# PReLU from PSUM, a one-column product as a tensor-scalar operation, and a new planned order of the first phase, in a pooled attention with feed-forward kernel

## The chip, the cores and the metric

The kernel runs on one core of a Trainium2 chip. The metric is the device time of one execution in microseconds (us). The engines are TensorE (PE; PEld is its weight load), VectorE (DVE), ScalarE (ACT), GpSimd (POOL) and SyncE (SP), which issues every DMA of this kernel. SBUF is the on-chip memory that all engines read; PSUM is the memory into which PE writes its products, in banks of 512 float32 columns.

## The reference

An attention whose keys and values are means of 8 neighbouring positions is followed by a feed-forward layer with PReLU (a slope `alpha` for each hidden feature).

```python
# q, k, v: (8, 8, 576, 64) float32
k_p = k.reshape(B, H, Sp, pool, D).mean(axis=3)      # pool = 8, Sp = 72
v_p = v.reshape(B, H, Sp, pool, D).mean(axis=3)
scores = scale * np.matmul(q, k_p.transpose(0, 1, 3, 2))
scores = scores - np.max(scores, axis=-1, keepdims=True)
attn = np.exp(scores)
attn = attn / (np.sum(attn, axis=-1, keepdims=True) + 1e-09)
x = np.matmul(attn, v_p)                             # then (4608, 512)

h = x @ w_in                                         # (512, 2048)
g = np.maximum(h, 0.0) + alpha * np.minimum(h, 0.0)
return (g @ w_out).astype(np.float32)                # (2048, 512)
```

## The kernel before

**Tiling.** The 4608 tokens are cut into nine chunks of 512 tokens. Every product is made of float16 halves: an operand is scaled by a power of two and split into a high part (ACT writes it) and a low part (what is left, written by DVE or POOL), and three matmuls of 512 columns give high x low, low x high and high x high. A chunk takes 192 matmuls `h` for the first layer (16 tiles `f` of 12), and 192 matmuls `o` for the second (4 token tiles `i`, each 16 steps of 3).

**The attention of a chunk** (`attention`): keys and values are pooled, scaled and split (`ks`, `kbd`, `vs`, `v`), queries are split (`q`), then come scores, row maxima, exponentials `e`, their normalisation (L532), the split into `apad` (L537 on ACT, L540 and L543 on POOL), a DMA transpose to `aT` for each of four token tiles, and the mix `x` (L605), which ACT and DVE split into the chunk's activation (L562, L566).

**The first layer of a tile** `f`: the matmuls fill one of two PSUM banks `h` (L769 to L771); ACT copies it, scaled by `rp`, to an SBUF tile `t` (L775), of which there are four, shared with `ks`, `vs` and the outputs; DVE makes the PReLU in place, the larger of `alpha` times `t` and `t` (L779); ACT writes its high part `g` (L786), POOL its low part (L789).

**The weights** arrive as 64-bit words, two words of 32 bits for each value, 8 tiles of 1 MB for each layer, into buffers `big`, of which there are twelve for all loads. `convert` turns a tile into float16 parts: ACT shifts the lower words (L641) and scales the upper ones into `v` (L651, L655; for three tiles of w1 POOL does it, L645), DVE joins three low bits (L665) and the sign (L669), each over 128 x 1024, ACT takes the high part (L688, L693), and POOL or DVE the low part (L707 on POOL for w1; L696 on DVE for 13 halves of w2, L702 on POOL for 3). The sign operation of every second tile frees a `big` buffer. No w2 low part can begin before the scale `s2` (L752), which needs the column maxima of all w2 tiles (L238), and so the last w2 load.

**What sets the order.** The first phase (`start`: chunk 0 as a whole, all weights, and the attention of chunk 1) is recorded in a `_Plan`: every operation has an engine, an assumed duration, what it comes after, buffers to take and give, and a rank from the table `RK`. The plan picks, engine by engine, what can start next and has the lowest rank, and issues the instructions in that order; PE gets idle matmuls where the plan sees a gap of more than 3.27 us. On the chip each engine runs its instructions in the issued order and waits for semaphores alone, not for planned times. For chunks 1 to 8 a loop issues the first layer with the next chunk's attention in between and then the second layer; there the compiler's scheduler sets the order, with second-layer products between first-layer tiles.

**What the change touches:** `RK`, `_Plan.add`, `start` and `emit`, `descale` (L581, the product of two scales and 2^-32 for each token, one column), `convert`, `scale_w1` (L718, L728), `ffn1_scaled`, `ffn1_prelu`, and the recording of the PReLU in `start`.

Of the kernel before, what the change touches and what calls it, by code (L numbers as in the profile page):

```python
# [72 lines left out]
class _Plan:  # L73
# [15 lines left out]
    def add(self, engine, us, emit, *after, rank=0.0, take=None, give=None):
        op = dict(engine=engine, us=us, emit=emit, after=after, rank=rank, n=len(self.ops),  # L90
                  take=take, give=(give,) if isinstance(give, str) else give or (), end=None)
        self.ops.append(op)
        return op

    def start(self, op, free):
        if any(d["end"] is None for d in op["after"]) or (op["take"] and not self.room[op["take"]]):
# [4 lines left out]
        return max(t)

    def emit(self):
        free, left = {}, list(self.ops)
        while left:
# [25 lines left out]
def pooled_attention_prelu_ffn(ctx: ExitStack, tc: tile.TileContext, qT, kT, vT, kN, vN, w1, w2, alpha, out):  # L131
# [441 lines left out]
    def descale(c, i):  # L573
# [4 lines left out]
        if key not in dss:  # L578
            ds = sml.tile([P, 1], F32, tag="ds", name="ds", bufs=4)
            for a, z, b in pr:  # L580
                nc.vector.scalar_tensor_tensor(out=ds[a:z], in0=eq[c, i // 2][a:z], scalar=2.0 ** -32,  # L581
                                               in1=ek[b][a:z], op0=ALU.mult, op1=ALU.mult)
# [50 lines left out]
    def convert(add, l, i, begin, sc, rank):  # L633
# [10 lines left out]
        if l == 1 and picked(i, RK["v_pool"], NF // 2):
            x = add("Pool", 2.4, lambda: nc.gpsimd.tensor_tensor(  # L645
                out=v(), in0=word(l, i, 1), in1=y1[:, 2 * i:2 * i + 2].broadcast_to([P, 2, 512]), op=ALU.mult),
                begin, rank=rank, take="v")
        elif l == 1:
            x = begin
            for j in range(2):  # L650
                x = add("ACT", 0.61, lambda j=j: nc.scalar.activation(  # L651
                    v()[:, j], word(l, i, 1)[:, j], AF.Copy, scale=y1[:, 2 * i + j:2 * i + j + 1]),
                    begin, x, rank=rank, take=None if j else "v")
        else:
            x = add("ACT", 1.15, lambda: nc.scalar.activation(  # L655
                v(), word(l, i, 1), AF.Copy, scale=2.0 ** -112 if wide else 1.0), begin, rank=rank, take="v")
        vi = lambda: v().bitcast(I32)
        if by_pool:
            x = add("Pool", 2.4, lambda: nc.gpsimd.tensor_tensor(
                out=vi(), in0=vi(), in1=eight.broadcast_to([P, 2, 512]), op=ALU.mult), x, rank=rank)  # L660
            x = add("DVE", 1.35, lambda: nc.vector.scalar_tensor_tensor(
                out=vi(), in0=word(l, i, 0).bitcast(I32), scalar=29, in1=vi(),
                op0=ALU.logical_shift_right, op1=ALU.bitwise_or), x, rank=rank)
        elif wide:
            x = add("DVE", 1.35, lambda: nc.vector.scalar_tensor_tensor(  # L665
                out=vi(), in0=vi(), scalar=3, in1=word(l, i, 0).bitcast(I32),
                op0=ALU.logical_shift_left, op1=ALU.bitwise_or), x, low, rank=rank)
        if wide:
            x = add("DVE", 1.5, lambda: nc.vector.scalar_tensor_tensor(  # L669
                out=vi(), in0=word(l, i, 1).bitcast(I32), scalar=-2 ** 31, in1=vi(),  # L670
                op0=ALU.bitwise_and, op1=ALU.bitwise_or), x, rank=rank, give="big" if i % 2 else None)
# [292 lines left out]
```

## Time and profile before

| what | us |
|---|---|
| median of three runs | 891.62 |
| lowest and highest of them | 888.89 and 892.07 |
| the profiled execution | 890.46 |
| its span, first to last instruction | 888.8 |
| PE, DVE, ACT, POOL busy in the span | 847.1, 452.9, 428.2, 400.5 |

The span has two parts that are read apart: the planned first phase, up to the mix of chunk 1, and the chunks after it. A mean over the whole span says little about either. A row of a group gives line, engine, operation, output and inputs with their shapes and the count, then busy us, mean ns of one, and the idle time ahead of it with what ended it. A row of the order in time gives start and duration in us; "x2" is two instructions merged into one row.

### The profile page before, as it was taken

Reading aid. Unit: us, or ns where it says so; the run is one execution under the profiler, and the core shown is the slowest. Engines: PE = TensorE matmul, PEld = TensorE weight load, DVE = VectorE, ACT = ScalarE, POOL = GpSimd, SP = SyncE. Lnnn points to the kernel's source line nnn. Section 1 sums busy time; section 2 is a strip of 40 time slices with the busy share of each in tenths; the row PEclk is TensorE's granted clock in tenths of the full one; section 3 lists DMA queues with packets and bytes.
Section 4 is the critical chain, followed back from the end, with each engine's and each line's share of the span. In section 5 each row is a group of like instructions: output and inputs, shape, how many; then the busy total and the mean of one; then the engine's idle time right before and its main releaser. Section 6 shows DMA issues by size and latency. Waiting matters only on the chain.

```text
span 888.8 us, 11503 instructions
## 1 busy us (share of the span) xinstructions
PE 847.1 (95%) x4447; PEld 411.1 (46%) x4447; DVE 452.9 (51%) x655; ACT 428.2 (48%) x724; POOL 400.5 (45%) x377
## 2 busy tenths in 40 slices
PE   6769997898999999999999999999999999999998
PEld 5444453344444544454445444544454444444443
DVE  4999999758415841583158315831583146112210
ACT  5967785555433643364336433643463346213330
POOL 1387948457714461456144614561456027202320
PEclk9879999999999999999999999999999999999999
DMA  9576312360621171117111611171115003100000
GB/s 339 198 158 268 124 51 51 75 202 9 157 96 40 25 182 56 39 28 192 43 39 28 178 57 38 29 198 37 39 28 119 36 13 70 26 36 12 1 25 24
DMA packets 93639, 74.75 MB, mean 84 GB/s; under 512 B 77040, under 2 KB 77616, under 8 KB 93584
## 3 DMA queue, kind: packets, MB, share of 16 engines
q1 hardware_dynamic: 93584, 74.01, 29.4%
q8 instruction: 35, 0.57, 0.3%
q14 instruction: 20, 0.16, 0.1%
HBM read 45.10 MB, written 9.44 MB: 61 GB/s over the span
## 4 chain that ended last, share of the span: by engine, by line
PE 81%; DVE 11%; POOL 3%; ACT 2%; DMA 2%; issue 2%; SPq 0%; POOLq 0%; ACTq 0%; DVEq 0%
PE o L815 13%; PE o L816 13%; PE o L817 13%; PE h L769 12%; PE h L770 12%; PE h L771 12%; PE x L605 2%; DVE v L665 2%; DVE t L779 2%; DVE m L238 1%; DMA vraw<-vT_dram 1%; PE s L595 1%; PE s L594 1%; PE s L596 1%; PE pl L283 1%
## 5 line engine op out<-in xcount | busy, mean ns | idle before, releaser
L789 POOL TENSOR_TENSOR g<-t,g 128x512 f16<-128x512 f32 x144 | 179.6, 1250 | 337.0 <-ACT g L786 337.0
L779 DVE SCALAR_TENSOR_TENSOR t<-t,al 128x512 f32<-128x512 f32 x144 | 140.5, 980 | 272.9 <-ACT t L775 266.1
L770 PE MATMUL h<-x,w 128*128 128x512 f16 x576 | 219.2, 381 | 2.4 <-DVE x L566 2.4
L769 PE MATMUL h<-x,w 128*128 128x512 f16 x576 | 219.1, 380 | 1.4 <-ACT o L805 1.4
L771 PE MATMUL h<-x,w 128*128 128x512 f16 x576 | 218.8, 380 | 0.0
L816 PE MATMUL o<-w,g 128*128 128x512 f16 x544 | 207.1, 381 | 4.4 <-POOL w L702 2.8
L815 PE MATMUL o<-w,g 128*128 128x512 f16 x544 | 206.7, 381 | 3.3 <-POOL g L789 2.8
L817 PE MATMUL o<-w,g 128*128 128x512 f16 x544 | 204.2, 381 | 0.0
L786 ACT CAST g<-t 128x512 f16<-128x512 f32 x144 | 88.4, 615 | 100.9 <-DVE t L779 100.5
L775 ACT ACTIVATE t<-h,rp 128x512 f32<-128x512 f32 x144 | 97.9, 681 | 67.1 <-PE h L771 63.7
L805 ACT ACTIVATE o<-o,os 128x512 f32<-128x512 f32 x34 | 23.2, 687 | 174.1 <-PE o L817 174.1
L815 PEld LDWEIGHTS <-g 128*128 128x128 f16 x576 | 56.5, 98 | 75.4 <-issue 6.0
L817 PEld LDWEIGHTS <-g 128*128 128x128 f16 x576 | 56.6, 98 | 73.8 <-issue 6.9
L771 PEld LDWEIGHTS <-w 128*128 128x128 f16 x576 | 56.5, 98 | 70.3 <-issue 3.5
L769 PEld LDWEIGHTS <-w 128*128 128x128 f16 x576 | 56.5, 98 | 68.1 <-issue 3.7
L816 PEld LDWEIGHTS <-g 128*128 128x128 f16 x576 | 56.5, 98 | 67.4 <-issue 2.1
L770 PEld LDWEIGHTS <-w 128*128 128x128 f16 x576 | 56.5, 98 | 65.4 <-issue 2.5
L463 POOL TENSOR_TENSOR vraw<-vraw 72x512 f32<-72x512 f32 (+1 forms) x56 | 58.9, 1069 | 56.7 <-DMA vraw<-vT_dram 45.8
L566 DVE SCALAR_TENSOR_TENSOR x<-x,xsc,x 128x512 f16<-128x512 f32 x36 | 25.8, 747 | 69.7 <-ACT x L562 69.7
L532 POOL TENSOR_TENSOR e<-e,sm 128x576 f32<-128x576 f32 x35 | 46.9, 1341 | 25.5 <-DVE sm L530 17.2
L537 ACT CAST apad<-e 128x576 f16<-128x576 f32 x72 | 44.8, 669 | 25.8 <-POOL e L532 18.0
L540 POOL TENSOR_TENSOR apad<-e,apad 128x448 f16<-128x448 f32 x36 | 41.7, 1158 | 3.3 <-ACT apad L537 3.1
(135 smaller groups left out, 886.0 us busy)
## 6 DMA issues: line engine op xcount, KB each, us to landing
w<-w_dram SPq DMA_DIRECT2D x16, 1024.0 KB
out_dram<-o SPq DMA_DIRECT2D x36, 256.0 KB
qraw<-qT_dram SPq DMA_DIRECT2D x17, 512.0 KB
vraw<-vT_dram SPq DMA_DIRECT2D x28, 288.0 KB
kraw<-kT_dram SPq DMA_DIRECT2D x12, 576.0 KB
kq<-kT_dram SPq DMA_DIRECT2D x2, 576.0 KB
nat<-kN_dram SPq DMA_DIRECT2D x2, 512.0 KB
nat<-vN_dram SPq DMA_DIRECT2D x2, 512.0 KB
```

The costliest lines, as they stand in the source:

```text
L463: nc.gpsimd.tensor_tensor(out=o, in0=y, in1=z, op=ALU.add)
L532: x = add("DVE" if i in on_dve else "Pool", us, lambda ex=ex, sm=sm, eng=eng: eng.tensor_tensor(out=ex(), in0=ex(), in1=sm().broadcast_to( ...
L769: nc.tensor.matmul(ps, w[:, 1, ks_], x[:, 0], start=(n == 0), stop=False)
L770: nc.tensor.matmul(ps, w[:, 0, ks_], x[:, 1], start=False, stop=False)
L771: nc.tensor.matmul(ps, w[:, 0, ks_], x[:, 0], start=False, stop=(n == NK - 1))
L775: nc.scalar.activation(t, hps.pop((c, f)), AF.Copy, scale=rp[:, f:f + 1])
L779: nc.vector.scalar_tensor_tensor(out=t, in0=t, scalar=al[:, f:f + 1], in1=t, op0=ALU.mult, op1=ALU.max)
L786: nc.scalar.copy(out=g[:, 0], in_=t)
L789: nc.gpsimd.tensor_tensor(out=g[:, 1], in0=t, in1=g[:, 0], op=ALU.subtract)
L815: nc.tensor.matmul(ps, g[:, 1, ts_], w[:, 0], start=(f == 0), stop=False)
L816: nc.tensor.matmul(ps, g[:, 0, ts_], w[:, 1], start=False, stop=False)
L817: nc.tensor.matmul(ps, g[:, 0, ts_], w[:, 0], start=False, stop=(f == NF - 1))
```

## The change

1. **PReLU.** ACT still copies `h`, scaled by `rp`, to `t`. DVE now takes its product from the PSUM bank itself, times a new column `ra` = `rp` x `alpha`, and the larger of that and `t` goes to `t`. The bank is so free only after the PReLU, where ACT's copy freed it. `ra` lies in the buffer of `m1`, and a POOL product for each of four groups of columns makes it.
2. **Scale product.** In `descale` the one-column product is a tensor-scalar operation, its second factor a scalar read from a column, where it was a scalar-tensor-tensor operation.
3. **Planner.** Every POOL operation and the DVE operations marked `two` (two tensors in SBUF, or a tensor-scalar form) share one `port`: in the plan one of them starts only when the last has ended. Many assumed durations are smaller.
4. **Table.** `RK` has new numbers. No scaling of w1 runs on POOL any more (`v_pool` was 3), four of eight w1 low parts run on DVE (`lo_dve` 0 to 4), all 16 w2 low halves run on DVE (`w2_dve` 13 to 16), and both halves of the early key pooling run on DVE (`k_pool` 1 to 0). A variant of `convert` that works in PSUM is added and is chosen for no tile (`ps1` and `ps2` are 0).

```diff
-RK = dict(k_pool=1, sh1_pool=0, sh2_pool=0, v_pool=3, s_pool=0, w2_dve=13, lo_dve=0, l1=392.23, step=2.57,
+RK = dict(k_pool=0, ps1=0, ps2=0, s_pool=0, w2_dve=16, lo_dve=4, l1=296.52, step=20.04, l2=536.5, mx1=19.17,
...
-    def add(self, engine, us, emit, *after, rank=0.0, take=None, give=None):
+    def add(self, engine, us, emit, *after, rank=0.0, take=None, give=None, two=False):
...
+                  two=two or engine == "Pool")
...
+        if op["two"]:
+            t.append(self.port)
         return max(t)
...
+            if op["two"]:
+                self.port = t + op["us"]
...
-                nc.vector.scalar_tensor_tensor(out=ds[a:z], in0=eq[c, i // 2][a:z], scalar=2.0 ** -32,
-                                               in1=ek[b][a:z], op0=ALU.mult, op1=ALU.mult)
+                nc.vector.tensor_scalar(out=ds[a:z], in0=eq[c, i // 2][a:z], scalar1=2.0 ** -32,
+                                        scalar2=ek[b][a:z], op0=ALU.mult, op1=ALU.mult)
...
-        if l == 1 and picked(i, RK["v_pool"], NF // 2):
-            x = add("Pool", 2.4, lambda: nc.gpsimd.tensor_tensor(
-                out=v(), in0=word(l, i, 1), in1=y1[:, 2 * i:2 * i + 2].broadcast_to([P, 2, 512]), op=ALU.mult),
-                begin, rank=rank, take="v")
...
-        x = add("DVE" if dve else "Pool", 1.5 if dve else 2.4, lambda: (nc.vector if dve else nc.gpsimd).tensor_tensor(
-            out=part(1), in0=v(), in1=part(0), op=ALU.subtract), x, rank=rank + RK[f"lo{l}"], give="v")
+        x = add("DVE" if dve else "Pool", 1.25 if dve else 2.3, lambda: (nc.vector if dve else nc.gpsimd).tensor_tensor(
+            out=part(1), in0=v(), in1=part(0), op=ALU.subtract), x, rank=rank + RK[f"lo{l}"], give="v", two=dve)
...
+        x = add("Pool", 0.2, lambda: nc.gpsimd.tensor_tensor(
+            out=rp[:, fs], in0=rp[:, fs], in1=sg[:, fs], op=ALU.mult), x, scaled["al"], rank=rank + 4)
         return y_, add("Pool", 0.2, lambda: nc.gpsimd.tensor_tensor(
-            out=rp[:, fs], in0=rp[:, fs], in1=sg[:, fs], op=ALU.mult), x, scaled["al"], rank=rank + 4)
+            out=ra[:, fs], in0=rp[:, fs], in1=al[:, fs], op=ALU.mult), x, rank=rank + 4)
...
-        nc.scalar.activation(t, hps.pop((c, f)), AF.Copy, scale=rp[:, f:f + 1])
+        nc.scalar.activation(t, hps[c, f], AF.Copy, scale=rp[:, f:f + 1])
...
-        nc.vector.scalar_tensor_tensor(out=t, in0=t, scalar=al[:, f:f + 1], in1=t, op0=ALU.mult, op1=ALU.max)
+        nc.vector.scalar_tensor_tensor(out=t, in0=hps.pop((c, f)), scalar=ra[:, f:f + 1], in1=t,
+                                       op0=ALU.mult, op1=ALU.max)
...
-            x = add("ACT", 0.69, lambda f=f: ffn1_scaled(0, f), x, rs[f], rank=rank + RK["sc"], take="f", give="h")
+            x = add("ACT", 0.69, lambda f=f: ffn1_scaled(0, f), x, rs[f], rank=rank + RK["sc"], take="f")
+            x = add("DVE", 0.76, lambda f=f: ffn1_prelu(0, f), x, rank=rank + RK["pre"], give="h")
             rd.append(x)
-            x = add("DVE", 1.25, lambda f=f: ffn1_prelu(0, f), x, rank=rank + RK["pre"])
```

The order moves at three places that matter below. Lines of the changed file differ: there L659 and L662 are the join and the sign operation, L775 is the PReLU, L701 the low part of w1, L712 the scale steps of w1, and `m_122` is the buffer of `m1` and `ra`.

First, POOL in the first phase, from its first product of the w1 scales on; `apad` is the split of a token tile of chunk 0. Before:

```order
L728 TENSOR_TENSOR rp<-rp,sg 128x2
L645 TENSOR_TENSOR v<-w_199,y_127 128x1024
L532 TENSOR_TENSOR e<-e,sm 128x576
L540 TENSOR_TENSOR apad_96<-e,apad_96 128x8x56
L543 TENSOR_TENSOR apad_96<-e,apad_96 128x8x16
L540 TENSOR_TENSOR apad_97<-e,apad_97 128x8x56
L543 TENSOR_TENSOR apad_97<-e,apad_97 128x8x16
L471 MEMSET vm 128x1
L728 TENSOR_TENSOR rp<-rp,sg 128x4
L707 TENSOR_TENSOR w_136<-v,w_136 128x2x512
L532 TENSOR_TENSOR e<-e,sm 128x576
L707 TENSOR_TENSOR w_136<-v,w_136 128x2x512
```

And in the changed kernel:

```order
L722 TENSOR_TENSOR rp<-rp,sg 128x2
L724 TENSOR_TENSOR m_122<-rp,al 128x2
L722 TENSOR_TENSOR rp<-rp,sg 128x4
L724 TENSOR_TENSOR m_122<-rp,al 128x4
L543 TENSOR_TENSOR apad_96<-e,apad_96 128x8x56
L546 TENSOR_TENSOR apad_96<-e,apad_96 128x8x16
L535 TENSOR_TENSOR e<-e,sm 128x576
L543 TENSOR_TENSOR apad_97<-e,apad_97 128x8x56
L546 TENSOR_TENSOR apad_97<-e,apad_97 128x8x16
L535 TENSOR_TENSOR e<-e,sm 128x576
L474 MEMSET vm 128x1
L701 TENSOR_TENSOR w_134<-v,w_134 128x2x512
```

The w1 scaling (L645) and one of the two w1 low parts (L707) ahead of the last tiles' splits are gone from POOL.

Second, DVE from the last split of chunk 0's activation on (`m_125`, and `m_123` after, are the maxima of w2 tiles, `w_272`, `w_282` tiles of w1). Before:

```order
L566 SCALAR_TENSOR_TENSOR x_688<-x,xsc,x_688 128x512
L238 TENSOR_REDUCE m_125<-w_664 128x2
L669 SCALAR_TENSOR_TENSOR v<-w_272,v 128x1024
L779 SCALAR_TENSOR_TENSOR t<-t,al 128x512
L238 TENSOR_REDUCE m_125<-w_686 128x2
L238 TENSOR_REDUCE m_125<-w_707 128x2
L779 SCALAR_TENSOR_TENSOR t<-t,al 128x512 x2
L238 TENSOR_REDUCE m_125<-w_732 128x2
L665 SCALAR_TENSOR_TENSOR v<-v,w_282 128x1024
```

And in the changed kernel, with `w_217` and `w_241` the fourth and fifth tile of w1 and `w_671` the first of w2:

```order
L569 SCALAR_TENSOR_TENSOR x_699<-x,xsc,x_699 128x512
L662 SCALAR_TENSOR_TENSOR v<-w_217,v 128x1024
L659 SCALAR_TENSOR_TENSOR v<-v,w_241 128x1024
L775 SCALAR_TENSOR_TENSOR t<-h,m_122,t 128x512
L662 SCALAR_TENSOR_TENSOR v<-w_241,v 128x1024
L712 TENSOR_SCALAR rp<-e_121 128x6
L241 TENSOR_REDUCE m_123<-w_671 128x2
L775 SCALAR_TENSOR_TENSOR t<-h,m_122,t 128x512
L241 TENSOR_REDUCE m_123<-w_697 128x2
L775 SCALAR_TENSOR_TENSOR t<-h,m_122,t 128x512
L241 TENSOR_REDUCE m_123<-w_717 128x2
L712 TENSOR_SCALAR y_125<-rp 128x6
```

At the split DVE now stands four joins and signs and three scale steps further back in the conversion of w1, and does them behind it.

Third, DVE in chunk 2, from the reduction of the next chunk's key maxima to the split of its queries. Before:

```order
L208 TENSOR_REDUCE pt<-pm 128x3
L213 TENSOR_SCALAR pr<-pt 128x3
L229 TENSOR_SCALAR e<-pr 128x3
L234 TENSOR_SCALAR s<-e 128x3
L581 SCALAR_TENSOR_TENSOR ds<-e 128x1
L581 SCALAR_TENSOR_TENSOR ds<-e 64x1 x2
L581 SCALAR_TENSOR_TENSOR ds<-e 128x1
L779 SCALAR_TENSOR_TENSOR t<-t,al 128x512
L425 SCALAR_TENSOR_TENSOR kbd_95<-ks,s,kbd_95 64x4x72 x2
L442 SCALAR_TENSOR_TENSOR q_2473<-qraw,s,q_2473 128x1024
L442 SCALAR_TENSOR_TENSOR q_2475<-qraw,s,q_2475 128x1024
```

And in the changed kernel:

```order
L216 TENSOR_SCALAR pr<-pt 128x3
L775 SCALAR_TENSOR_TENSOR t<-h,m_122,t 128x512
L232 TENSOR_SCALAR e<-pr 128x3
L237 TENSOR_SCALAR s<-e 128x3
L584 TENSOR_SCALAR ds<-e 128x1
L584 TENSOR_SCALAR ds<-e 64x1 x2
L584 TENSOR_SCALAR ds<-e 128x1
L428 SCALAR_TENSOR_TENSOR kbd_95<-ks,s,kbd_95 64x4x72 x2
L445 SCALAR_TENSOR_TENSOR q_2538<-qraw,s,q_2538 128x1024
L445 SCALAR_TENSOR_TENSOR q_2540<-qraw,s,q_2540 128x1024
L775 SCALAR_TENSOR_TENSOR t<-h,m_122,t 128x512
```

The PReLU that stood between the scale products and the key split has moved ahead of e, and the whole preparation of keys and queries now stands between two PReLUs.

Ahead of the mix of chunk 1, PE now has all 192 second-layer products of chunk 0; before, the last 12 of them stood behind it.

More of the change, by code (lines that the diff above doesn't have):

```diff
@@ L86, in __init__ @@
         self.fill = fill
-        self.ops, self.room = [], {k: n * [0.0] for k, n in room.items()}
-    def add(self, engine, us, emit, *after, rank=0.0, take=None, give=None):
+        self.ops, self.room, self.port = [], {k: n * [0.0] for k, n in room.items()}, 0.0
+    def add(self, engine, us, emit, *after, rank=0.0, take=None, give=None, two=False):
         op = dict(engine=engine, us=us, emit=emit, after=after, rank=rank, n=len(self.ops),
-                  take=take, give=(give,) if isinstance(give, str) else give or (), end=None)
+                  take=take, give=(give,) if isinstance(give, str) else give or (), end=None,
+                  two=two or engine == "Pool")
         self.ops.append(op)
@@ L428, in attention @@
                 h = add("ACT", 0.53, hi, scs[0], rank=rank)
-                kd.append(add("DVE", 0.6, lo, h, *kd[2 * i:], rank=rank, give="f" if j else None))
+                kd.append(add("DVE", 0.6, lo, h, *kd[2 * i:], rank=rank, give="f" if j else None, two=True))
         qd = {}
@@ L444, in attention @@
                     op0=ALU.mult, op1=ALU.subtract),
-                    h, *([qd[1]] if end else []), rank=rk,
+                    h, *([qd[1]] if end else []), rank=rk, two=True,
                         give="big" if end else "aT" if early and a + w == HC else None)
@@ L532, in attention @@
             x = add("DVE" if i in on_dve else "Pool", us, lambda ex=ex, sm=sm, eng=eng: eng.tensor_tensor(
-                out=ex(), in0=ex(), in1=sm().broadcast_to([P, 2, 4, SP]), op=ALU.mult), x, rank=rk)
+                out=ex(), in0=ex(), in1=sm().broadcast_to([P, 2, 4, SP]), op=ALU.mult), x, rank=rk, two=True)
             ev_ = lambda ex=ex: ex().rearrange("p b h s -> p (b h) s")
@@ L638, in convert @@
         v = once(lambda: wp.tile([P, 2, 512], F32, tag="v", name="v", bufs=ROOM["v"]))
-        by_pool = wide and picked(i, RK[f"sh{l}_pool"], NF // 2)
-        if wide and not by_pool:
-            low = add("ACT", 1.2, lambda: nc.scalar.activation(
+        ps = once(lambda: ps_s.tile([P, 2, CH], F32, tag="s", name="vw"))
+        by_ps = wide and picked(i, RK[f"ps{l}"], NF // 2)
+        u, kind = (ps, "S") if by_ps else (v, "v")
+        if wide:
+            low = add("ACT", 1.15, lambda: nc.scalar.activation(
@@ L650, in convert @@
             for j in range(2):
-                x = add("ACT", 0.61, lambda j=j: nc.scalar.activation(
-                    v()[:, j], word(l, i, 1)[:, j], AF.Copy, scale=y1[:, 2 * i + j:2 * i + j + 1]),
-                    begin, x, rank=rank, take=None if j else "v")
+                x = add("ACT", 0.66, lambda j=j: nc.scalar.activation(
+                    u()[:, j], word(l, i, 1)[:, j], AF.Copy, scale=y1[:, 2 * i + j:2 * i + j + 1]),
+                    begin, x, rank=rank, take=None if j else kind)
@@ L654, in convert @@
         else:
             x = add("ACT", 1.15, lambda: nc.scalar.activation(
[L656 to L667, printed above, removed]
@@ L668, in convert @@
-        if wide:
-            x = add("DVE", 1.5, lambda: nc.vector.scalar_tensor_tensor(
-                out=vi(), in0=word(l, i, 1).bitcast(I32), scalar=-2 ** 31, in1=vi(),
-                op0=ALU.bitwise_and, op1=ALU.bitwise_or), x, rank=rank, give="big" if i % 2 else None)
+                u(), word(l, i, 1), AF.Copy, scale=2.0 ** -112 if wide else 1.0), begin, rank=rank, take=kind)
+        if wide:
+            x = add("DVE", 1.22, lambda: nc.vector.scalar_tensor_tensor(
+                out=u().bitcast(I32), in0=u().bitcast(I32), scalar=3, in1=word(l, i, 0).bitcast(I32),
+                op0=ALU.logical_shift_left, op1=ALU.bitwise_or), x, low, rank=rank, two=not by_ps)
+            x = add("DVE", 1.22, lambda: nc.vector.scalar_tensor_tensor(
+                out=v().bitcast(I32), in0=word(l, i, 1).bitcast(I32), scalar=-2 ** 31, in1=u().bitcast(I32),
+                op0=ALU.bitwise_and, op1=ALU.bitwise_or), x, rank=rank, two=not by_ps,
+                take="v" if by_ps else None, give=(*(["big"] if i % 2 else []), *(["S"] if by_ps else [])))
@@ L718, in small @@
             return add("DVE", 0.2, lambda: nc.vector.tensor_scalar(
-                out=out, in0=in0, scalar1=s1, scalar2=s2_, op0=op0, op1=op1), x, rank=rank)
+                out=out, in0=in0, scalar1=s1, scalar2=s2_, op0=op0, op1=op1), x, rank=rank, two=True)
         x = add("DVE", 0.2, lambda: floor2(r[0], e1[:, fs], wide), x, rank=rank)
```

23 lines of the change are left out of this document (10 added, 13 removed).

## The prediction

> **What bounds the kernel now.** I read PE's busy slices first, then busy time by stage, then the chain of work that ended last, and then the groups of the first stage and its order in time.
>
> ```profile
> PE   6769997898999999999999999999999999999998
> 0.00:67.00 67.00, 44.68 (x251) 30.49 (x252) 52.67 (x99) 48.08 (x102) 32.29 (x35) 0.87 0.74 233
> 67.00:119.00 52.00, 47.85 (x234) 23.09 (x234) 49.90 (x52) 39.91 (x57) 42.88 (x25) 0.97 0.43 167
> 119.00:159.00 40.00, 33.26 (x190) 16.32 (x189) 39.63 (x50) 28.68 (x66) 27.56 (x27) 0.92 0.20 54
> 270.00:360.00 90.00, 90.00 (x487) 43.26 (x486) 43.47 (x63) 40.69 (x66) 39.31 (x41) 1.00 0.28 74
> ```
>
> A window row gives its bounds and length, then busy time of PE, PE's weight loads, DVE, ACT and POOL, and the granted clock. There are two regimes. From about 210 us on PE has no gap (90.00 of 90.00), so nothing that only shortens DVE, ACT or POOL work there can move the end. In the first phase DVE has no gap (49.90 of 52, 39.63 of 40), and PE waits for it. A gain must come from the first phase, up to the second mix:
>
> ```profile
> 63.23 1.93 PE L605 MATMUL x<-aT,v 88*64 88x512 f16 x16 [1.37 <-DVE v L665]
> 67.06 2.71 DVE L566 SCALAR_TENSOR_TENSOR x<-x,xsc,x 128x512 f16<-128x512 f32 x4
> 171.31 1.03 PE x L605 x12
> ```
>
> The first mix runs at 63.2, DVE splits its result at 67.1, and the mix of chunk 1 starts at 171.3. Behind that PE is full, and whatever 171.3 moves, the end moves.
>
> **Why DVE is full.** Much of its time is blocked time:
>
> ```profile
> L665 DVE SCALAR_TENSOR_TENSOR v<-v,w 128x1024 int32<-128x1024 int32 x16 | 25.4, 1589 | 0.0
> L669 DVE SCALAR_TENSOR_TENSOR v<-w,v 128x1024 int32<-128x1024 int32 x16 | 21.8, 1364 | 0.0
> L779 DVE SCALAR_TENSOR_TENSOR t<-t,al 128x512 f32<-128x512 f32 x16 | 17.7, 1129 | 0.4 <-ACT t L775 0.4
> L696 DVE SCALAR_TENSOR_TENSOR w<-v,s,w 128x512 f16<-128x512 f32 x13 | 15.1, 1174 | 0.9 <-ACT w L693 0.8
> 122.61 1.21 DVE L669 SCALAR_TENSOR_TENSOR v<-w,v 128x1024 int32<-128x1024 int32 x1
> 123.74 0.74 DVE L696 SCALAR_TENSOR_TENSOR w<-v,s,w 128x512 f16<-128x512 f32 x1
> 109.86 3.84 POOL L789 TENSOR_TENSOR g<-t,g 128x512 f16<-128x512 f32 x3
> 112.71 2.07 DVE L665 SCALAR_TENSOR_TENSOR v<-v,w 128x1024 int32<-128x1024 int32 x1
> ```
>
> The first four rows are means of the first 172 us. At 122.6, with POOL idle, the 1024 form takes 1.13 us from start to start and the 512 form 0.74. At 112.7 the same 1024 form stands at 2.07, since POOL's third g ends at 113.70; 1.08 us later it is done. So a DVE operation with both tensors in SBUF waits for POOL's running one. The blocked time over the first phase is 16 x (1.59 - 1.13) + 16 x (1.36 - 1.13) + 13 x (1.17 - 0.74) = 16.6 us, and 16 x (1.13 - 0.74) = 6.2 us in the PReLU.
>
> **The change, part by part**, between the first split and the second mix, against the profiled execution's own 890.46 us (span 888.8 and 1.7 around it). The median of the three runs shown is 891.62, 1.2 above it.
>
> PReLU. It now reads PSUM and SBUF. The nearest row has that form and size:
>
> ```profile
> L566 DVE SCALAR_TENSOR_TENSOR x<-x,xsc,x 128x512 f16<-128x512 f32 x4 | 2.7, 736 | 0.0
> L779 DVE SCALAR_TENSOR_TENSOR t<-t,al x144: 732/752/2489, 72.6 to 858.3; 128x512 f32<-128x512 f32 x144
> ```
>
> I take 0.74, the two rows agreeing (0.736 from PSUM, 0.732 the fastest from SBUF); the bounds are 0.73 and the old 1.13. That is 16 x 0.39 = **-6.2 us**. [...]
>
> One-column scale product, now a tensor-scalar form:
>
> ```profile
> L581 DVE SCALAR_TENSOR_TENSOR ds<-e 128x1 f32<-128x1 f32 x4 | 4.6, 1151 | 0.0
> 149.36 1.37 DVE L581 SCALAR_TENSOR_TENSOR ds<-e 128x1 f32<-128x1 f32 x1
> 137.07 1.22 DVE L581 SCALAR_TENSOR_TENSOR ds<-e 128x1 f32<-128x1 f32 x1
> L213 DVE TENSOR_SCALAR pr<-pt 128x1 f32<-128x1 f32 x11 | 1.7, 153 | 0.4
> L213 DVE TENSOR_SCALAR pr<-pt 128x3 f32<-128x3 f32 x7 | 8.1, 1158 | 0.2
> ```
>
> Two of the products in the stretch took 1.37 and 1.22. I take 0.15 from the one-column row, bounds 0.15 and 1.15 from the three-column one: 2 x 1.15 = **-2.3 us**. [...]
>
> Earlier start. Ahead of the last transposes of chunk 0 POOL loses one scaling and one of two subtractions:
>
> ```profile
> 27.57 2.35 POOL L645 TENSOR_TENSOR v<-w,y 128x1024 f32<-128x1024 f32 x1 [9.65 <-DVE y L718]
> 28.06 1.87 DVE L581 SCALAR_TENSOR_TENSOR ds<-e 128x1 f32<-128x1 f32 x1
> 48.47 2.12 POOL L707 TENSOR_TENSOR w<-v,w 128x1024 f16<-128x1024 f32 x1
> 58.66 2.10 DVE L718 TENSOR_SCALAR rp<-e 128x6 int32<-128x6 int32 x1
> 63.02 1.86 DVE L718 TENSOR_SCALAR rp<-rp 128x6 int32<-128x6 int32 x1
> ```
>
> Without L645 the product at 28.06 is not blocked (1.7), and POOL saves 2.1 on its chain; with the shorter collisions I put the mix 5 us earlier. On DVE four 1024 operations (4 x 1.13) and the two rows at 58.66 and 63.02 leave the place ahead of the split, 8.5 us, so DVE is no longer 2 us late for it: the split starts about **7 us** earlier. Bounds 4 and 9.
>
> Work moved behind the split. By the order, the stretch now holds 25 of the 1024 operations where it held 21 (4 x 1.13), 16 w2 subtractions for 13 (3 x 0.74), four w1 subtractions taken from POOL, one key reduction more, and three scale steps (3 x 0.16). The w1 subtraction is not shown on DVE; it has two SBUF tensors of 1024, so 1.13 to 1.59, and I take 1.13, POOL's work around it being thinner. The reduction:
>
> ```profile
> 110.82 1.35 DVE L372 TENSOR_REDUCE ks<-kq 128x144 f32<-128x1152 f32 x1
> ```
>
> Sum: 4.5 + 2.2 + 4.5 + 1.35 + 0.5 = **+13.1 us**.
>
> Blocked time of the rest. In the stretch 34 exposed operations become 45, while POOL's work falls by an estimated 13 us (three or four passes of 2.1, three half passes, three key additions) of some 58, blocked time left out of its 42.88 + 27.56 = 70.4 us busy from 67 to 159. The 16.6 us lie on 45 operations, 0.37 each, which makes 34 x 0.37 = 12.6 before and 45 x 0.37 x 45 / 58 = 12.9 after: **0**. This is where I choose: the planner's rule for shared ports could halve it (-6 to -8), and the denser order could raise it.
>
> So the second mix starts at 171.3 - 7 - 6.2 - 2.3 + 13.1 = 168.9, **-2.4 us**. The last 12 FFN2 products now stand ahead of it (12 products at 0.216, a price shown below, are 2.6 us less behind it), but they filled PE while x was split; I keep half, **-1.3**.
>
> Later chunks. The h bank is now freed by DVE, not ACT, so PE waits for DVE where the queue is long:
>
> ```profile
> 373.62 1.30 DVE L213 TENSOR_SCALAR pr<-pt 128x3 f32<-128x3 f32 x1
> 374.96 1.07 DVE L229 TENSOR_SCALAR e<-pr 128x3 int32<-128x3 int32 x1
> 376.07 0.34 DVE L234 TENSOR_SCALAR s<-e 128x3 int32<-128x3 int32 x1
> 377.60 1.21 DVE L425 SCALAR_TENSOR_TENSOR kbd<-ks,s,kbd 64x288 f16<-64x288 f32 x2
> 378.85 2.48 DVE L442 SCALAR_TENSOR_TENSOR q<-qraw,s,q 128x1024 f16<-128x1024 f32 x2
> 359.07 0.38 PE L769 MATMUL h<-x,w 128*128 128x512 f16 x1
> 364.03 0.38 PE L771 MATMUL h<-x,w 128*128 128x512 f16 x1
> ```
>
> Between the fourth and fifth PReLU of a chunk now stand e, s, the products, kbd and q: 1.07 + 0.34 + 0.6 + 1.21 + 2.48 = 5.7 us. The two PE rows are the first and the last of 24 products without a gap, 4.96 / 23 = 0.216 us each; PE meanwhile has 12 h and 12 o products, 24 x 0.216 = 5.2. That is up to 0.5 us in each of seven chunks; the o products that the order puts between h tiles cover most, so **+1.0** (0 to 3.5).
>
> Sum: 890.5 - 2.4 - 1.3 + 1.0 = 887.8, **888 us**, a change of -0.3%.
>
> **The rivals.** 1. *The order keeps DVE and POOL apart.* For it: fewer POOL passes, and the plan starts no POOL operation beside a two-tensor DVE one. Against: nothing on the chip holds the engines to the plan, and the rows drift by more than one operation. Price: 16.6 halved, -8.3: 880 us. PE allows it, as it has room in the last stage before the mix, 0.85 us busy of 4 and a clock of 0.58 there:
>
> ```profile
> 152.00:156.00 4.00, 0.85 (x2) 0.21 (x2) 4.00 (x7) 3.38 (x6) 3.62 (x3) 0.58 0.69 131
> ```
>
> 2. *The last w2 tile comes later.* Its load waits for the buffer that the last w1 tile's sign operation frees:
>
> ```profile
> 95.40 2.18 DVE L669 SCALAR_TENSOR_TENSOR v<-w,v 128x1024 int32<-128x1024 int32 x1
> 97.73 4.88 DMA w<-w_dram
> 114.70 0.22 DVE L752 SCALAR_TENSOR_TENSOR s<-e,w2s,sg 128x16 f32<-128x16 f32 x1
> ```
>
> From the split to that operation stood 24 DVE instructions (22.5 us unblocked, 30.6 as run); now 39 stand there, 35.8 unblocked. Starting 7 us earlier they end at 96 unblocked, at 103 if a fifth is added, 5 us after 97.6. From there everything up to s2 and the first w2 product is late by that: the mix falls at about 176, and the sum is 895 us. It decides from 2 us of blocked time per ten of work on.
>
> 3. *The held h bank stalls PE in every chunk.* If e and the q split wait for POOL as at 374.96, 2 us are missing instead of 0.5, seven times, less what o products cover: about +12 on the sum, 900 us. It decides from 5.2 us between two PReLUs on.
>
> 4. *The PReLU is still blocked*, because its second tensor lies in SBUF: +6, 894 us; L566 never shows it. It is in the range, with little weight.
>
> **How the numbers follow.** Forecast (888, with -0.5% to +0.5%) 0.39; rival 1 0.33; rival 2 0.14; rival 3 0.10; rival 4 0.04. About 0.5%, 4.5 us, is what a measurement of this kernel can tell from no change. Faster by more: rival 1 and a little of the forecast's lower edge, 0.35. Slower by more: rivals 2 and 3 and part of 4 and of the upper edge, 0.27. Within: 0.38. The range is 878 to 899: it takes in rival 1 to its full price, rival 2 and the bounds of start and moved work; the likeliest case alone is 884 to 893.
>
> **What would show it.** PReLU near 0.74 in the first phase as later; one-column products near 0.15; first split near 60; the last w2 load starting near 98; the second mix near 169; 1024 operations still at 1.4 to 1.6 in the mean (below 1.3 speaks for rival 1); PE without gaps from 270 to 720 (gaps in front of h products speak for rival 3). The forecast is wrong if the mix falls outside 164 to 174 or a late chunk loses over 1 us.

## The result: 921.36 us, and the profile after

| kernel | median, us | lowest to highest | ratio to before, 95% interval |
|---|---|---|---|
| before | 891.15 (4 runs) | 888.89 to 892.07 | |
| changed | 921.36 (4 runs) | 918.21 to 921.94 | 1.0336 (1.0305 to 1.0366) |

The change makes the kernel 3.4% slower. The profiled execution took 921.94 us, its span is 920.2. Two stray executions among the experiments, of 1793.85 us (the scale product alone) and 2816.56 us (the run with one more rule), are left out of the ratios below. First the busy slices of PE from the page of the changed kernel, then its windows (columns as in the prediction):

```profile
PE   6789899789999999999998999999999999999998
```
```profile
67.00:119.00 52.00, 46.14 (x234) 22.81 (x233) 50.19 (x55) 38.18 (x54) 31.74 (x27) 0.97 0.39 142
119.00:159.00 40.00, 39.00 (x238) 20.63 (x236) 37.01 (x56) 30.64 (x68) 14.34 (x14) 1.00 0.09 29
270.00:360.00 90.00, 85.84 (x456) 40.61 (x455) 38.95 (x63) 39.69 (x64) 37.05 (x41) 0.98 0.27 72
```

The slices hide what happened: a slice is 23 us long, and one or two microseconds do not change its digit. The window of a late chunk shows it: 85.84 of 90.00 us busy where the kernel before had 90.00, at a mean clock of 0.98 instead of 1.00. DVE and POOL have less to do there than before, and PE still waits. The view of PE's waits from 205 to 900 us (line, what it waited for, us in total, times, longest) names two releasers, first in the changed kernel:

```profile
PE h L765 <- DVE t L775: 9.7, 5, 2.3
PE o L812 <- POOL g L786: 8.6, 5, 2.2
```

The same view of the kernel before has only this:

```profile
PE o L815 <- ACT o L805: 0.2, 1, 0.2
```

To see where the time goes, count the first- and second-layer products in the order of their starts (3456 of them) and ask how much later the one with N products ahead of it starts than in the kernel before. The first column of times is its start before; the others are the lag, from PE's instructions in the profiled executions of the changed kernel and of four experiments that are described below.

| products ahead | before, us | changed | PSUM in chunk 0 alone | g first | old form in f 3 to 5 | both edits |
|---|---|---|---|---|---|---|
| 384 | 177.3 | -1.5 | -1.2 | +0.1 | -0.9 | -2.7 |
| 480 | 198.2 | +6.5 | +5.8 | +7.9 | +7.1 | +4.8 |
| 576 | 226.7 | +1.8 | +1.0 | +3.1 | +2.3 | 0.0 |
| 1056 | 338.3 | +10.8 | +1.0 | +5.9 | +11.5 | +1.5 |
| 1536 | 447.2 | +16.8 | +1.0 | +8.0 | +16.4 | +3.0 |
| 2112 | 580.9 | +23.2 | +1.0 | +11.9 | +19.6 | +5.5 |
| 2688 | 713.6 | +29.4 | +1.0 | +14.2 | +23.2 | +6.8 |
| 3264 | 843.0 | +29.9 | +1.0 | +14.7 | +23.6 | +7.2 |

Up to the second mix the changed kernel is 1.5 us ahead, at product 576 it is 1.8 behind, and then it loses 28 us in the chunks that prepare a later chunk's attention. From product 2688 on it loses almost nothing more.

**The first wait: the h bank.** DVE in chunk 2 of the changed kernel (start, duration, operation):

```profile
287.93 0.74 DVE L775 SCALAR_TENSOR_TENSOR t<-h,m,t 128x512 f32<-128x512 f32 x1
288.59 2.79 DVE L232 TENSOR_SCALAR e<-pr 128x3 int32<-128x3 int32 x1
291.42 0.34 DVE L237 TENSOR_SCALAR s<-e 128x3 int32<-128x3 int32 x1
291.67 0.77 DVE L584 TENSOR_SCALAR ds<-e 128x1 f32<-128x1 f32 x4
292.36 1.36 DVE L428 SCALAR_TENSOR_TENSOR kbd<-ks,s,kbd 64x288 f16<-64x288 f32 x2
294.09 2.48 DVE L445 SCALAR_TENSOR_TENSOR q<-qraw,s,q 128x1024 f16<-128x1024 f32 x2 [0.37 <-ACT q L441]
296.49 0.74 DVE L775 SCALAR_TENSOR_TENSOR t<-h,m,t 128x512 f32<-128x512 f32 x1
```

POOL and PE at the same time:

```profile
288.52 1.15 POOL L786 TENSOR_TENSOR g<-t,g 128x512 f16<-128x512 f32 x1
290.21 1.14 POOL L786 TENSOR_TENSOR g<-t,g 128x512 f16<-128x512 f32 x1
291.32 1.53 POOL L466 TENSOR_TENSOR vs<-vraw 72x128 f32<-72x128 f32 x4
```
```profile
294.98 0.38 PE L814 MATMUL o<-w,g 128*128 128x512 f16 x1
297.28 0.38 PE L765 MATMUL h<-x,w 128*128 128x512 f16 x1 [1.93 <-DVE t L775]
```

Between the fourth and the fifth PReLU lie 8.56 us from start to start, and the fifth is done after 9.3. From the start of the fourth PE still had 15 h and 18 o products, 33 x 0.216 = 7.1 us, and then both h banks were full: the next h product waits 1.93 us until the PReLU of 296.49 has read its bank. The step e (L232) stands at 2.79 us instead of the 1.07 that the prediction took for it; it does so in each of chunks 2 to 6 (2.79 us), and the interval is 8.55 or 8.56 in each. The run of POOL operations beside e ends with the g at 290.21 + 1.14 = 291.35, and e is done at 288.59 + 2.79 = 291.38. In the kernel before the blocked instruction was another one (DVE, and then POOL):

```profile
281.63 2.49 DVE L779 SCALAR_TENSOR_TENSOR t<-t,al 128x512 f32<-128x512 f32 x1 [1.79 <-ACT t L775]
286.34 1.08 DVE L229 TENSOR_SCALAR e<-pr 128x3 int32<-128x3 int32 x1
```
```profile
286.24 1.15 POOL L789 TENSOR_TENSOR g<-t,g 128x512 f16<-128x512 f32 x1
```

There the PReLU sat through POOL's run, 2.49 us, and e came later and waited for the end of one g only, at 286.24 + 1.15 = 287.39. Now the PReLU does not wait, e starts beside an earlier g and sits through three POOL operations in its place; and what stands behind e is the instruction that frees PE's bank. In the run with PSUM in chunk 0 alone, e is back at 1.08 us in all five chunks. Whether the shorter PReLU or the compiler's new order (the PReLU ahead of e) brings e to that place was not separated.

**The second wait: the last g of a chunk.** POOL at the end of chunk 2, the load that it waits for (from the chain that ended last), and PE, all of the changed kernel:

```profile
335.34 1.15 POOL L786 TENSOR_TENSOR g<-t,g 128x512 f16<-128x512 f32 x1 [4.30 <-ACT g L783]
341.50 2.49 POOL L466 TENSOR_TENSOR vraw<-vraw 72x512 f32<-72x512 f32 x2 [5.01 <-DMA vraw<-vT_dram]
343.95 1.15 POOL L786 TENSOR_TENSOR g<-t,g 128x512 f16<-128x512 f32 x1
```
```profile
331.98 9.45 DMA vraw<-vT_dram
```
```profile
345.16 0.61 PE L812 MATMUL o<-w,g 128*128 128x512 f16 x1 [2.23 <-POOL g L786]
```

And POOL of the kernel before at the same place:

```profile
328.90 1.16 POOL L789 TENSOR_TENSOR g<-t,g 128x512 f16<-128x512 f32 x1 [1.28 <-ACT g L786]
335.96 3.64 POOL L463 TENSOR_TENSOR vraw<-vraw 72x512 f32<-72x512 f32 x4 [5.91 <-DMA vraw<-vT_dram]
```

Before, all 16 low parts g of the chunk stood on POOL ahead of the first pooling of the next values. Now two or three poolings stand ahead of the sixteenth g, and they wait for a load that lands at 341.5. The second layer of the chunk needs that g, and PE waits 2.23 us for it. The orders show it; what follows are letters for POOL's operations in chunk 2, g for a low part, v for a pooling into `vraw`, s for one into `vs`, e for a normalisation, up to the sixteenth g:

```
before   vvvvgvgvvgvgssssggggeggegegegggg | vvvv...
changed  vgvgvvgvgssssgggeggeggeeggggvvg | vvgvg...
```

**The third part: the clock.** The windows around that wait (columns as above; the last but two is the granted clock):

```profile
343.00:345.00 2.00, 0.00 (x0) 0.00 (x0) 0.75 (x1) 0.64 (x1) 2.00 (x2) 1.00 0.00 0
345.00:348.00 3.00, 2.84 (x10) 0.91 (x12) 0.00 (x0) 0.69 (x2) 1.24 (x3) 0.52 0.00 0
```

After the wait PE runs at half clock for 3.41 us, which costs 1.7 us more. This follows four of the waits (2.09 to 2.33 us); a fifth of 2.08 us and all shorter ones are not followed by it.

The parts add up: 9.7 us of waits for the bank, 7.7 for g (8.6 less one of 0.9 in the last chunk), 4 x 1.7 = 6.8 at half clock, and 3.4 in the mixes: from 270 to 860 us the mixes keep PE busy for 15.2 us instead of 11.8 (some of it at half clock), since the order now cuts them, nine pieces in the whole program before and eighteen now, with second-layer products between. That is 27.6, where the table has 29.9 - 1.8 = 28.1.

### The profile page after: what moved, and what is told of

It reads as the page before. It is cut to its first block, busy times and chain, and to the rows that moved or that the text cites. A ratio compares the mean times of both kernels' runs of the same rounds, so it can differ in the third digit from the quotient of the medians.

```text
span 920.2 us, 11648 instructions
## 1 busy us (share of the span) xinstructions
PE 863.9 (94%) x4510; PEld 418.3 (45%) x4510; DVE 419.6 (46%) x662; ACT 432.0 (47%) x727; POOL 344.5 (37%) x368
## 3 DMA queue, kind: packets, MB, share of 16 engines
q1 hardware_dynamic: 93584, 74.01, 28.1%
## 4 chain that ended last, share of the span: by engine, by line
PE 67%; DVE 10%; DMA 6%; issue 6%; POOL 4%; ACT 4%; SPq 2%; POOLq 0%; ACTq 0%; DVEq 0%
PE o L812 10%; PE o L813 10%; PE o L814 10%; PE h L765 10%; PE h L766 9%; PE h L767 9%; DMA vraw<-vT_dram 4%; POOL g L786 2%; DVE t L775 2%; PE idle L834 2%; DVE e L232 1%; SPq L253 1%; PE x L608 1%; DMA nat<-kN_dram 1%; DVE v L662 1%
## 5 line engine op out<-in xcount | busy, mean ns | idle before, releaser
L786 POOL TENSOR_TENSOR g<-t,g 128x512 f16<-128x512 f32 x144 | 170.4, 1184 | 383.5 <-ACT g L783 381.2
L775 DVE SCALAR_TENSOR_TENSOR t<-h,m,t 128x512 f32<-128x512 f32 x144 | 106.9, 743 | 304.5 <-ACT t L771 299.3
L765 PE MATMUL h<-x,w 128*128 128x512 f16 x576 | 221.1, 386 | 15.5 <-DVE t L775 12.0
L766 PE MATMUL h<-x,w 128*128 128x512 f16 x576 | 221.8, 385 | 0.9 <-DVE x L569 0.9
L767 PE MATMUL h<-x,w 128*128 128x512 f16 x576 | 221.6, 385 | 0.0
L771 ACT ACTIVATE t<-h,rp 128x512 f32<-128x512 f32 x144 | 97.7, 682 | 131.9 <-PE h L767 104.8
L466 POOL TENSOR_TENSOR vraw<-vraw 72x512 f32<-72x512 f32 (+1 forms) x56 | 54.4, 984 | 69.7 <-DMA vraw<-vT_dram 51.5
L535 POOL TENSOR_TENSOR e<-e,sm 128x576 f32<-128x576 f32 x35 | 40.2, 1148 | 48.6 <-DVE sm L533 35.3
L543 POOL TENSOR_TENSOR apad<-e,apad 128x448 f16<-128x448 f32 x36 | 37.3, 1036 | 15.9 <-ACT apad L540 15.9
```

The costliest lines, as they stand in the source:

```text
L466: nc.gpsimd.tensor_tensor(out=o, in0=y, in1=z, op=ALU.add)
L765: nc.tensor.matmul(ps, w[:, 1, ks_], x[:, 0], start=(n == 0), stop=False)
L766: nc.tensor.matmul(ps, w[:, 0, ks_], x[:, 1], start=False, stop=False)
L767: nc.tensor.matmul(ps, w[:, 0, ks_], x[:, 0], start=False, stop=(n == NK - 1))
L771: nc.scalar.activation(t, hps[c, f], AF.Copy, scale=rp[:, f:f + 1])
L775: nc.vector.scalar_tensor_tensor(out=t, in0=hps.pop((c, f)), scalar=ra[:, f:f + 1], in1=t, op0=ALU.mult, op1=ALU.max)
```

## The experiments

**The PReLU from PSUM in chunk 0 alone.** The bank is freed by ACT again in chunks 1 to 8; the first phase keeps its order.

```diff
-        nc.vector.scalar_tensor_tensor(out=t, in0=hps.pop((c, f)), scalar=ra[:, f:f + 1], in1=t,
+        t, ps = hs[c, f], hps.pop((c, f))
+        p = c == 0
+        nc.vector.scalar_tensor_tensor(out=t, in0=ps if p else t, scalar=(ra if p else al)[:, f:f + 1], in1=t,
```

> The changed kernel with the PReLU's product from PSUM in chunk 0 alone; in chunks 1 to 8 it is the old in-place form, so that ACT's copy frees the h bank again. The first phase is issued in the same order. Theory: the loss lies in the late chunks, where PE waits (five times for the PReLU, 9.7 us; four times for the last g of a chunk, 7.7 us) and each wait of 2.1 us or more is followed by 3.4 us at half clock (four times, 1.7 us each). All that goes: 921.4 - 24 to 28 = 893 to 897 us, and PE has no gap from 270 to 720. Rival (the new table or the first phase costs the time, the late waits follow from it): 915 us or more.

Measured: 890.81 us, ratio to before 1.0014 (1.0000 to 1.0028). All of the late loss is gone, a little more than expected. The late window has no gap:

```profile
270.00:360.00 90.00, 90.00 (x487) 43.13 (x486) 42.36 (x63) 40.13 (x65) 40.80 (x41) 1.00 0.28 75
```

So the new table, the planner's rule, the scale product and the PReLU of chunk 0 together leave the time about where it was, and the change's whole loss lies in the PReLU of the later chunks.

**The PReLU from PSUM in the late chunks alone**, in the kernel before: the same edit with `p = c > 0`, and the four POOL products for `ra`.

> The kernel before, with the PReLU's product from PSUM in chunks 1 to 8 alone; old table, old planner, old scale product, old PReLU in chunk 0 (four small POOL products for the new column are added). Theory: the loss comes with this alone: 891.2 + 24 to 28 = 915 to 919 us, with the same two waits in the late chunks. Rival (table or first phase): 891 us.

Measured: 918.66 us, ratio 1.0332 (1.0291 to 1.0373). The loss comes whole, without any other part of the change, with the same two waits (12.7 us for the PReLU, 9.3 for g).

**The g first.** The pooling of a later chunk's values is queued on POOL behind the last g of the chunk before:

```diff
+            last["g"] = nc.gpsimd.tensor_tensor(out=g[:, 1], in0=t, in1=g[:, 0], op=ALU.subtract)
...
+        g_last = last["g"]
...
-                  tc.issue_after(last["o"].ins)):
+                  tc.issue_after(last["o"].ins), tc.issue_after(g_last.ins)):
```

> The changed kernel, with the pooling of a later chunk's values queued on POOL behind the last low part g of the chunk before; the PReLU stays as changed. Theory of two separate waits: the four waits of second-layer products for g go, 7.7 us and two steps of half clock, 3.4 us: 910 us (907 to 914), while the five waits for the PReLU stay. Rival (the g is late only because its h tile was late, so the place in POOL's queue is of no account): 918 to 921 us.

Measured: 906.32 us, ratio 1.0189 (1.0163 to 1.0215): 15.0 us less than the changed kernel, four more than expected and just outside the expected range. PE's waits from 205 us on:

```profile
PE h L765 <- DVE t L775: 7.6, 5, 1.8
PE o L812 <- POOL g L786: 0.9, 1, 0.9
```

The waits for g of the late chunks are gone. The five for the bank stay, but are shorter (at most 1.8 us), and none is followed by half clock; so all four steps of the clock went, not two.

**The old form in tiles 3 to 5** of chunks 1 to 8, `p = c == 0 or f not in (3, 4, 5)`, so that ACT frees the bank beside which DVE prepares keys and queries.

> The changed kernel with the old in-place PReLU for tiles 3, 4 and 5 of chunks 1 to 8, beside which DVE prepares keys and queries; the other tiles take the product from PSUM. Theory of two separate waits: the five waits for the PReLU go, 9.7 us and two steps of half clock, 3.4 us: 908 us (904 to 912), while the waits for g stay, since POOL's order still has the pooling ahead of the last g. Rival (the waits for g follow from the waits for the PReLU): 897 us or less.

Measured: 912.55 us (907.62 to 915.25), ratio 1.0251 (1.0210 to 1.0292): 8.8 us less, where 13 were expected, and just outside the expected range. The waits for g stay, and the five waits for the PReLU are replaced by shorter ones for ACT's copy of the same bank, though e still takes 2.80 us in each of the five chunks:

```profile
PE o L814 <- POOL g L788: 10.1, 5, 3.4
PE h L766 <- ACT t L772: 5.2, 5, 1.2
```

**Both edits at once**; 13 of 16 tiles of a chunk still take the product from PSUM.

> The changed kernel with both edits at once: values pooled on POOL behind the last low part g of the chunk before, and the old in-place PReLU for tiles 3, 4 and 5 of chunks 1 to 8; the other 13 tiles of a chunk still take the product from PSUM. If the two waits are all that the late chunks lost and are separate, the gains add: 921.4 - 15.0 - 8.8 = 897.6, of which five waits of about 1 us for ACT's copy are left (5.2 us in the run with the old form in tiles 3 to 5), so 896 to 898. Rival 1 (one wait replaces the other): 906, as with the edit of POOL's order alone. Rival 2 (PSUM in the other tiles costs nothing and no wait is left): 891.

Measured: 900.31 us, ratio 1.0134 (1.0108 to 1.0160). The gains nearly add: 921.4 - 900.3 = 21.1, beside 15.0 + 8.8 = 23.8. Of the 9.5 us that are left to the run with PSUM in chunk 0 alone, 3.4 are waits for ACT's copy, 0.9 one for g, and 2.8 mixes (14.6 us busy instead of 11.8, in twenty pieces). These make 7.1 us; the profiled executions of the two runs, from which they are read, lie 7.0 us apart (898.86 and 891.83), and the other 2.5 us are the distance of these executions from their medians.

**The scale product alone**, in the kernel before, every engine's order the same:

```diff
-                nc.vector.scalar_tensor_tensor(out=ds[a:z], in0=eq[c, i // 2][a:z], scalar=2.0 ** -32,
-                                               in1=ek[b][a:z], op0=ALU.mult, op1=ALU.mult)
+                nc.vector.tensor_scalar(out=ds[a:z], in0=eq[c, i // 2][a:z], scalar1=2.0 ** -32,
+                                        scalar2=ek[b][a:z], op0=ALU.mult, op1=ALU.mult)
```

> The kernel before with the one-column scale product as a tensor-scalar operation and nothing else; every engine's order is the same. Theory of the prediction: two products of 1.15 us too long lie on DVE between the first split and the second mix, so 2.3 us go, 887 to 888 us beside 889.5, ratio 0.997 to 0.998. Rival: DVE's gain is taken by the next wait (POOL's operations and the weights' loads are no earlier), ratio 0.9995 to 1.0005.

Measured: 888.16 us beside 889.54, ratio 0.9978 (0.9963 to 0.9993), which is 2.0 us (0.6 to 3.3) and agrees with the term of the prediction. In the profile the products take 0.20 us (four of 202 ns in the mean before 172 us); its one execution was slower than the median, so that the gain is shown by the times alone.

**The PReLU from PSUM in chunk 0, old order**: the kernel before with `p = c == 0`.

> The kernel before with the PReLU's product from PSUM in chunk 0 alone; the order of DVE, ACT, PE and SP is that of before, POOL has four small products more. Theory of the prediction: 16 x 0.39 = 6.2 us of blocked time go from DVE ahead of the second mix, 883 to 885 us, ratio 0.993 to 0.995, the PReLU near 0.74. Rival: the PReLU gets short, but the time moves to the DVE operations behind it, which now meet POOL's running operation or a later engine: 889 us, ratio 0.998 to 1.002, with the 1024-column forms longer than 1.59 and 1.36.

Measured: 889.72 us beside 889.54, ratio 1.0002 (0.9987 to 1.0017): nothing. The PReLU itself did what was forecast, from the groups up to 172 us:

```profile
L782 DVE SCALAR_TENSOR_TENSOR t<-h,m,t 128x512 f32<-128x512 f32 x16 | 11.9, 747 | 7.2 <-ACT t L777 7.1
```

17.7 us of DVE became 11.9, and DVE then waited 7.2 us, nearly all for ACT's copies, which waited for PE's h products (9.1 us from 66 to 116, where the kernel before has 5.5). The kernel before shows why, in the chain that ended last and in its windows:

```profile
72.56 2.17 DVE t L779
...
109.67 0.77 DVE t L779
```
```profile
68.00:108.00 40.00, 40.00 (x179) 17.71 (x178) 38.13 (x33) 30.43 (x42) 33.77 (x19) 0.97 0.52 204
```

Fourteen of the sixteen PReLUs of chunk 0 lie between 72.6 and 110.4 (the last two, at 114.85 and 115.58, took 0.74 us each and had nothing to gain), and from 68 to 108 PE ran its products without a gap, all of them first-layer products. DVE was full there, and PE was full too. (The run is not quite the one edit: the banks come free later too, and PE waits 2.72 us for the last PReLU ahead of its idle products. What the PReLU would bring without that is not shown. Its profiled execution, 894.09 us, was the slowest of twelve.)

**The new order without PSUM**: the changed kernel with `p = False`; every engine's order is that of the run with PSUM in chunk 0 alone.

> The changed kernel with the old in-place PReLU in all chunks, chunk 0 too; table, planner, orders and scale product as changed, every engine's order that of the run with the product from PSUM in chunk 0 alone (890.8). Theory of the prediction: the PReLU of chunk 0 is blocked again, up to 16 x 0.39 = 6.2 us: 894 to 897. Rival 1 (the new order keeps DVE and POOL apart by itself): the in-place form is not blocked either, 891. Rival 2 (giving the bank free earlier, by ACT, is worth more): below 889.

Measured: 899.43 us, ratio 1.0101 (1.0081 to 1.0122): 8.6 us slower than with PSUM in chunk 0 by the medians, 5.3 by the spans of the two profiled executions (895.0 and 889.7; this one was the fastest of six). So in this order the PReLU is worth about the 6.2 us of the prediction or more. Its group up to 172 us:

```profile
L776 DVE SCALAR_TENSOR_TENSOR t<-t,al 128x512 f32<-128x512 f32 x16 | 19.7, 1231 | 3.5 <-ACT t L771 3.5
```

The PSUM form takes 742 ns there, so 16 x 0.49 = 7.8 us are blocked time. A part of it is taken from other DVE operations: the join and the sign operation take 1.22 and 1.27 us in the mean here, 1.32 and 1.38 with PSUM in chunk 0. And here DVE is the bound, since four low parts of w1 are DVE's now and the h products wait for them. PE's waits from 60 to 180 us, with the old form and with PSUM in chunk 0:

```profile
PE h L765 <- DVE w L701: 10.6, 3, 5.6
```
```profile
PE h L765 <- DVE w L701: 3.5, 2, 3.2
```

**PSUM in chunk 0 and one more rule**: as the first experiment, and in chunk 1 the pooling of chunk 2's values stands behind the first low parts g of chunk 1 on POOL.

```diff
+                        with tc.issue_after(last["g"].ins) if c == 2 else nullcontext():
                             nc.gpsimd.tensor_tensor(out=o, in0=y, in1=z, op=ALU.add)
```

> As the run with the product from PSUM in chunk 0 alone (890.8), and in chunk 1 the pooling of chunk 2's values is queued on POOL behind the first low parts g of chunk 1. There PE waited 3.5 us at 194 us for a g that stood behind the pooling, and 3.4 us at half clock followed. Theory: that goes, 3.5 + 1.7 = 5.2 us: 885 to 887 us, faster than both kernels. Rival: the next late thing takes it (the scores and the third mix, since the values come later): 889 to 892.

Measured: 887.72 us beside 889.54, ratio 0.9972 (0.9958 to 0.9986), 2.5 us by the ratio: the fastest median of all, about level with the scale product alone. The wait was to be worth five against the first experiment; the medians show 890.81 - 887.72 = 3.1, the spans of the two profiled executions 889.7 - 885.0 = 4.7. The wait of 3.5 us for g is gone, and PE waits 1.7 us for ACT's copies, where it waited 0.4.

## Why the prediction was wrong

It said 888 us with a range from 878 to 899; 921.36 lies outside, and the sign is wrong. Step by step:

- **Later chunks, +1.0 (0 to 3.5): this is the step that failed**, by 27 us. Two things were wrong in it. The interval between two PReLUs was worked out from single durations of the kernel before, with e at 1.07 (5.7 us in all); it is 8.56 from start to start. Of the 2.86 us that were missing, 1.72 are e beside POOL's run, 0.66 the PReLU's own time, which the sum left out, 0.37 a wait for ACT at the query split (in chunk 2), and the rest is small. PE's side of the comparison was wrong the other way: it had not 24 products but 31 to 35 from the start of the fourth PReLU on, so that "the o products that the order puts between h tiles cover most" was too cautious. At 5.7 us there would have been no wait, and at 8.56 it is 1.6 to 2.3 us; the interval alone decided. Rival 3 described the wait rightly, with e waiting for POOL and 2 us missing, at a chance of 0.10. Its 2 us came near in part by luck, since it set them against 5.2 us of products where PE had 7.1; its price of 12 us stands beside 9.7 us of waits and two steps of the clock. The other half was in no rival: the order of POOL in the late chunks was not read. There the sixteenth g had moved behind poolings that wait for a load, which the rows of the order would have shown. And no term had the half clock that follows such waits, 6.8 us, or the mixes in pieces, 3.4 us.
- **PReLU 0.74, right as a duration** (741 ns in the mean of sixteen; 747 in the old order). Its -6.2 us does not hold by itself: it is nothing in the old order, where PE was full beside those PReLUs (the statement that PE waits for DVE throughout the first phase was wrong from 68 to 108), and 5.3 to 8.6 us in the new order.
- **Scale product, -2.3: right within what can be told**, 0.19 us each in the changed kernel and 2.0 us for it alone.
- **Earlier start.** First mix, split, s2, first second-layer product and second mix of the changed kernel:

```profile
59.79 0.41 PE L608 MATMUL x<-aT,v 88*64 88x512 f16 x2
62.19 2.07 DVE L569 SCALAR_TENSOR_TENSOR x<-x,xsc,x 128x512 f16<-128x512 f32 x3 [2.93 <-ACT x L565]
119.65 0.23 DVE L748 SCALAR_TENSOR_TENSOR s<-e,w2s,sg 128x16 f32<-128x16 f32 x1
121.61 0.38 PE L812 MATMUL o<-w,g 128*128 128x512 f16 x1
169.77 0.25 PE L608 MATMUL x<-aT,v 88*64 88x64 f16 x4
173.35 2.54 PE L608 MATMUL x<-aT,v 88*64 88x448 f16 x28 [3.33 <-DMA aT<-apad]
```

  The split is 4.9 us earlier (67.06 before), inside the bounds of 4 and 9. The last w2 load is issued at 102.2 (97.7 before) and s2 is 5.0 us later (114.70 before), as rival 2 had it, but the mix was not late by that: from s2 to the first products of the mix the changed kernel needs 50.1 us, the one before 56.0 (they start at 170.67).
- **Blocked time of the rest: 0 was too high.** The groups of the changed kernel up to 172 us:

```profile
L662 DVE SCALAR_TENSOR_TENSOR v<-w,v 128x1024 int32<-128x1024 int32 x16 | 22.0, 1380 | 0.1
L659 DVE SCALAR_TENSOR_TENSOR v<-v,w 128x1024 int32<-128x1024 int32 x16 | 21.0, 1320 | 0.5 <-ACT v L652 0.3
L690 DVE SCALAR_TENSOR_TENSOR w<-v,s,w 128x512 f16<-128x512 f32 x16 | 13.7, 882 | 0.7 <-ACT w L687 0.7
L701 DVE TENSOR_TENSOR w<-v,w 128x1024 f16<-128x1024 f32 x4 | 6.7, 1696 | 0.0
```

  By the same free durations that is 16 x 0.25 + 16 x 0.19 + 16 x 0.14 + 4 x 0.57 = 11.6 us on 52 operations, beside 16.6 on 45. That is 5.0 us less, where rival 1 had 8.3, and the moved w1 low part costs 1.70, not 1.13.
- **Second mix at 168.9:** its first products start at 169.77, but the rest waits 3.33 us for the last transpose. By product 576 the gain of the first phase is spent; the first experiment ends 1.3 us above the kernel before, at the edge of what it can tell.

The first phase and the order at the second mix, -3.7 us in the sum, came to +1.3 (0.0 to 2.5) in the first experiment. That this too is close to nothing is in part luck: s2 came later, the rest was less blocked, and a wait for the last transpose and one for a g in chunk 1 took the gain. The time was decided where the text said in its first paragraph that nothing can be gained. What can't be gained can be lost: a PE without gaps only says that whatever frees its banks and feeds it is in time in that order.

## What to carry to other kernels

Reading a PSUM bank with one more instruction, on another engine, moved the point at which it comes free to that engine's queue (from 205 us on PE waited 9.7 us for DVE's PReLU, where it had waited for none): list what stands ahead of the new last reader in that queue, with the blocked durations that hold after the change, and compare it with the work that PE has in hand. Where a scheduler orders the program, read its order on every engine for each stage that the changed instruction runs in, above all what waits for a load ahead of something that PE needs. Before a shortened operation is counted as a gain, look whether PE has gaps just beside it, in a window as short as the stage, not in the mean of a phase.

## What the runs showed of the hardware

- Waits of PE were often dearer than their length. After 200 us, in the traces of the kernels before and changed, of PSUM in the late chunks alone and of the old form in tiles 3 to 5, there are 14 waits between 2.0 and 3.4 us; nine are followed by half clock for 3.41 us or twice that, and no shorter one is. In the kernels before and changed these are six waits: five, of 2.09 to 2.57 us, are followed by 3.41 us at a granted clock of 0.50, which costs 1.7 us each, and the one of 2.08 is not. In the new order without PSUM one of 2.46 us, at 201.4, is not either, so the length of the wait alone does not settle it.
- The PReLU with its product from PSUM took 750 ns for 128 x 512 in the median of 144 in the changed kernel, the one from SBUF 752 in the kernel before.
- Blocked time passed to another DVE operation: freed from it, the PReLU in chunk 2 stood at 0.74 instead of 2.49 us, and a tensor-scalar step of three columns at 2.79 instead of 1.08.
